# Two transposes ahead of two loads, and 22 idle products that become 14 longer ones

## The chip, the cores and the metric

The kernel runs on one core of one Trainium2 chip. The core has five engines, each with a queue of its own that is worked off in order: TensorE (PE in the profile; PEld is its loading of weights), VectorE (DVE), ScalarE (ACT), GpSimd (POOL) and SyncE (SP), which computes nothing and issues DMA transfers. Sixteen DMA engines move the data. The metric is the device time of one execution in microseconds.

## The reference: what is computed

Eight batches, eight heads, 576 positions, 64 numbers a head. First a retention (an attention with decay instead of a softmax), then a layer of 512 to 2048 to 512 with a snake activation:

```python
scores = scale * np.matmul(q, k.transpose(0, 1, 3, 2))
Dmat = np.where(rel >= 0, gamma[:, None, None] ** rel[None, :, :], 0.0)
attn = np.matmul(scores * Dmat[None], v)      # gamma: one for each head
x = attn.transpose(0, 2, 1, 3).reshape(B * S, H * D)   # 4608 x 512
h = x @ w_in                                  # 4608 x 2048
s = np.sin(alpha * h)
out = (h + s * s / (alpha + 1e-09)) @ w_out   # 4608 x 512
```

All inputs and the output are float32; the kernel multiplies in float16.

## The kernel before, in words

**Attention.** The decay is split over q and k: each is multiplied by its factors while it is cast to float16 (*cast*, line 158), so that a mask of zeros and ones is all that is left for the scores. A batch's 576 positions are two halves of 256 (p = 0 and 1) and a rest of 64 that is done for pairs of batches at the end. Each half has two chunks of 128. Within a chunk the scores are computed (*scores*, line 362), masked on DVE (*masked*) and multiplied with v (*values*, line 392). Between chunks a state of k times v is handed on: *outer* (line 295) makes the products on PE, *evict* (line 317) copies them from PSUM to the tile `kvs` on ACT, *more* (line 350) adds the decayed state of the chunk before on POOL, and *to_state* (line 341) gives the float16 form that *add_states* (line 425) multiplies with q. There is one `kvs` for all batches, so the copy of batch 3's products must wait until batch 2's last state, chunk 3, has been read from it. *keep* (line 443) copies the result to the tile `xT`.

**The layer.** A block n is 512 positions of one batch. *project* (line 541) makes 128 of the 2048 columns of h with four products of 512 columns; *sine* on ACT, *square* on ACT, DVE or POOL, and *product* on DVE turn them into a slice of `gT`; *gemm2* (line 587) adds four such slices to 128 rows of the output, and *finish* (line 581) copies and stores them. Blocks 0, 1 and 2 are interleaved with the attention of batches 1, 2, 3 and 4 by a list written out by hand (lines 653 to 1124); from block 3 on a loop of 16 units does it, with batch n + 1's attention at fixed units.

**Order.** The program is under a manual schedule: every engine gets its instructions in the order in which the calls stand in the source, and waits only for data and for buffers. So the place of a *load* (line 137, a transfer of 512 KB issued by SP) is its place in SP's queue, and the place of a *cast* on POOL its place in POOL's queue. Buffers are given out in the order of the calls from strings of slots (lines 18 to 33): `raw`, the loaded float32 data, has six slots, `k16` four, `q16` three.

**Transposes.** Batches 0 and 1 transpose k and q on PE (*turn* and *take*). From batch 2 on this is done by DMA: *crossed* (line 213) issues a DMA transpose from SBUF to SBUF of one half of k or q, 128 x 1024 float16, on SP's queue, after the cast that it reads. *scores* reads the two results, `kT` and `qT`.

**Around the change.** In the hand-written list, line 979 casts batch 3's q (second half) on POOL and lines 988 and 989 its k (first half), also on POOL. Lines 994 to 997 load and cast batch 4's k (second half) and q (first half). Then come POOL's *more(3)* of batch 2 (line 998), the transposes of batch 3's second half (lines 999 and 1000) and PE's scores on them (lines 1001 and 1003), batch 2's *to_state(3)* on POOL (line 1004), and the transposes of batch 3's first half (lines 1008 and 1009), whose first use on PE is at line 1015, behind *outer* (line 1014); *evict* is line 1016.

**Idle products.** *keep_busy* (line 602) multiplies a tile of zeros with itself into a PSUM bank that nobody reads. Line 676 issues 22 such products of 128 columns while DVE casts batch 0's q; the transposes of that q on PE (line 681) stand behind them.

Of the kernel before, what the change touches and what calls it, by code (L numbers as in the profile page):

```python
# [35 lines left out]
def kernel(  # L36
# [77 lines left out]
    def halves(n):  # L114
        return slice(64 * n, 64 * n + 64)
# [10 lines left out]
    def place(tag, shape, dtype):  # L126

        name = tag + next(slot_of[tag])
        if name not in places:
            places[name] = work.tile(shape, dtype, tag=name, bufs=1, name=name)  # L130
        return places[name]
# [5 lines left out]
    def load(b, nm, p):  # L137
        if p < 2 and b >= HALVED and nm != "q":
            t_ = place("raw", [P, H, 2 * D], F32)
            for g in range(2):  # L140
                for r in range(2):
                    s0 = 256 * p + 128 * g + 64 * r
                    nc.sync.dma_start(
                        t_[halves(g), :, r * D : r * D + D], src[nm][b, :, s0 : s0 + 64, :].rearrange("h i d -> i h d")
                    )
        elif p < 2:
            t_ = place("raw", [P, H, 2 * D], F32)
            nc.sync.dma_start(  # L148
                t_, src[nm][b, :, 256 * p : 256 * p + 256, :].rearrange("h (i r) d -> i h (r d)", r=2)
            )  # L150
        else:
            if b % 2 == 0:
                raw[b, nm, 2] = work.tile([P, H, D], F32, tag="raws", bufs=3, name=nm + "s32")
            t_ = raw[b - b % 2, nm, 2]
            nc.sync.dma_start(t_[halves(b % 2)], src[nm][b, :, 512:576, :].rearrange("h i d -> i h d"))
        raw[b, nm, p] = t_
# [47 lines left out]
    def new_T(b, nm, p):  # L204
        if (b, nm, p) not in T:
            T[b, nm, p] = (
                place(nm + "T", [P, 8, P], F16)
                if p < 2
                else work.tile([P, 4, P], F16, tag=nm + "Ts", bufs=B // 2, name=nm + "Ts")
            )  # L210
        return T[b, nm, p]

    def crossed(b, p, nms="kq"):
        for nm in nms:
            x = half[b, nm, p]
            x = x.rearrange("p a r t d -> p (a r t d)") if p < 2 else x.rearrange("p a t d -> p (a t d)")
            nc.sync.dma_start_transpose(new_T(b, nm, p), x)
# [369 lines left out]
    def gemm2(n, u, tag, cols=slice(0, 512)):  # L587
        c, part = divmod(u, 4)
        if (n, c, cols.start) not in ops:
            ops[n, c, cols.start] = psum.tile([P, 512], F32, tag=tag, bufs=1, name="ops")  # L590
        for fk in range(4 * part, 4 * part + 4):
            matmul(  # L592
                ops[n, c, cols.start][:, cols], gT[n][:, fk, c * P : (c + 1) * P], w_out16[:, fk, cols],
                start=(fk == 0), stop=(fk == FC - 1), skip_group_check=True,
            )

    at = [Attention(b) for b in range(B)]
# [4 lines left out]
    def keep_busy(n, tag, m=512):  # L602
        idle = psum.tile([P, 512], F32, tag=tag, bufs=1, name="idle")
        for _ in range(n):
            matmul(idle[:, 0:m], zero[:, 0:P], zero[:, 0:m], start=True, stop=True)
# [46 lines left out]
    with tc.manual_schedule():  # L652
# [20 lines left out]
        at[0].take_sum(0, A_)  # L673
        at[0].to_state(0, A_)
        cast(0, "q", 0, V)
        keep_busy(22, "h2", 128)
        at[0].next_sum(1)
        at[0].to_state(1, A_)
        load(0, "k", 1)
# [311 lines left out]
        gemm2(1, 2, "h2")  # L991
        gemm2(1, 3, "h2")
        at[2].keep(0, V)
        load(4, "k", 1)
        cast(4, "k", 1, G_)
        load(4, "q", 0)
        cast(4, "q", 0, G_)
        at[2].more(3)
        crossed(3, 1, "k")
        crossed(3, 1, "q")  # L1000
        at[3].scores(1, 1, "m1")
        at[3].masked(1, 1)
        at[3].scores(1, 0, "m0")
# [252 lines left out]
```

## Time and profile before

| what | value |
|---|---|
| median of 3 runs | 311.7 us (311.09 to 312.0) |
| the profiled execution | 309.53 us |
| its span, first to last instruction | 307.8 us |
| PE busy | 291.3 us, 95% |
| POOL busy | 128.9 us, 42% |
| granted TensorE clock | 1.0 |
| moved by DMA | 49.98 MB, 162 GB/s on average |

The page gives busy time for each engine, the chain of work that ended last (followed back from the last instruction to whatever released it), and groups of instructions. Its other views give the waits of each engine by what ended them, the instructions in order of time, and the busy time in chosen stretches, with the number of instructions in brackets. In these rows a line such as L372 is a line of the source, `out<-in` names the tiles, SPq is SP's queue of DMA issues, and "issue" is a wait for which the profile shows no cause. Instructions that only wait or branch are not counted in the stretches.

### The profile page before, as it was taken

Reading aid. Unit: us, or ns where it says so; the run is one execution under the profiler, and the core shown is the slowest. Engines: PE = TensorE matmul, PEld = TensorE weight load, DVE = VectorE, ACT = ScalarE, POOL = GpSimd, SP = SyncE. Lnnn points to the kernel's source line nnn. Section 1 sums busy time; section 2 is a strip of 40 time slices with the busy share of each in tenths; the row PEclk is TensorE's granted clock in tenths of the full one; section 3 lists DMA queues with packets and bytes.
Section 4 is the critical chain, followed back from the end, with each engine's and each line's share of the span. In section 5 each row is a group of like instructions: output and inputs, shape, how many; then the busy total and the mean of one; then the engine's idle time right before and its main releaser. Section 6 shows DMA issues by size and latency. Waiting matters only on the chain.

```text
span 307.8 us, 7895 instructions
## 1 busy us (share of the span) xinstructions
PE 291.3 (95%) x3225; PEld 156.3 (51%) x3225; DVE 197.2 (64%) x281; ACT 193.3 (63%) x323; POOL 128.9 (42%) x149
## 2 busy tenths in 40 slices
PE   3879999999799999999999999799999999999995
PEld 1758555555355654554455445444455454444443
DVE  2867796968576876867665686556656746655600
ACT  3748877994278668665776577556774456555411
POOL 2767774467664556686159626833030000000000
PEclk9999999999999999999999999999999999999999
DMA  8999999999567398889799969966361121111132
GB/s 222 347 224 213 275 276 324 276 235 238 126 171 207 85 182 190 234 183 150 169 255 169 205 151 269 157 142 144 75 134 38 38 43 39 34 34 34 44 90 74
DMA packets 115620, 49.98 MB, mean 162 GB/s; under 512 B 71424, under 2 KB 110592, under 8 KB 115584
## 3 DMA queue, kind: packets, MB, share of 16 engines
q1 hardware_dynamic: 112064, 45.10, 63.1%
q0 software_dynamic: 2688, 4.19, 7.6%
q8 instruction: 25, 0.41, 0.6%
q10 hardware_dynamic: 832, 0.18, 0.4%
q14 instruction: 11, 0.09, 0.1%
HBM read 36.75 MB, written 9.44 MB: 150 GB/s over the span
## 4 chain that ended last, share of the span: by engine, by line
PE 82%; DMA 7%; issue 3%; POOL 2%; ACT 2%; DVE 2%; SPq 1%; POOLq 0%; DVEq 0%; ACTq 0%
PE ops L592 38%; PE hps L549 36%; PE o L414 2%; PE sc L372 2%; DMA raw<-in_k_dram 2%; DMA raw<-in_q_dram 2%; DMA raw<-in_v_dram 2%; PE kv L308 1%; ACT s L557 1%; DMA qT<-q 1%; POOL w_in L109 1%; SPq L148 1%; PE o L436 1%; DVE ret L384 1%; POOL k L194 1%
## 5 line engine op out<-in xcount | busy, mean ns | idle before, releaser
L592 PE MATMUL ops<-w_out,gT 128*128 128x512 f16 (+2 forms) x592 | 142.6, 374 | 0.1
L557 ACT ACTIVATE s<-hps,alpha_t 128x512 f16<-128x512 f32 x144 | 97.7, 685 | 69.4 <-PE hps L549 67.9
L573 DVE SCALAR_TENSOR_TENSOR gT<-ss,inva,hps 128x512 f16<-128x512 f16 x144 | 105.6, 745 | 52.5 <-ACT ss L566 47.9
L549 PE MATMUL hps<-xT,w_in 128*128 128x512 f16 (+1 forms) x544 | 126.9, 367 | 2.1 <-issue 2.0
L549 PEld LDWEIGHTS <-w_in 128*128 128x128 f16 x608 | 68.0, 114 | 58.2 <-issue 2.2
L592 PEld LDWEIGHTS <-gT 128*128 128x128 f16 x592 | 56.2, 98 | 63.0 <-issue 0.7
L568 DVE TENSOR_TENSOR ss<-s 128x512 f16<-128x512 f16 x62 | 34.9, 562 | 20.6 <-ACT s L557 20.0
L566 ACT ACTIVATE ss<-s 128x512 f16<-128x512 f16 x73 | 46.0, 631 | 1.4
L194 POOL TENSOR_TENSOR k<-raw,cn 128x1024 f16<-128x1024 f32 (+1 forms) x17 | 26.7, 1576 | 34.0 <-DMA raw<-in_k_dram 30.0
L119 ACT COPY osb<-ops 128x512 f32<-128x512 f32 (+1 forms) x33 | 19.2, 581 | 15.2 <-PE ops L592 13.8
L384 DVE TENSOR_TENSOR ret<-sc,mask 128x1024 f16<-128x1024 f32 x20 | 23.8, 1218 | 7.1 <-PE sc L372 7.1
L194 POOL TENSOR_TENSOR q<-raw,cn 128x1024 f16<-128x1024 f32 (+1 forms) x10 | 18.5, 1868 | 2.1 <-DMA raw<-in_q_dram 1.3
L353 POOL TENSOR_TENSOR s<-kvs,cn 128x256 f32<-128x256 f32 x21 | 13.7, 651 | 11.4 <-ACT kvs L119 11.3
L354 POOL TENSOR_TENSOR kvs<-s,kvs 128x256 f32<-128x256 f32 x21 | 16.0, 762 | 3.6 <-ACT kvs L119 2.2
L119 ACT CAST xT<-o 128x1024 f16<-128x1024 f32 (+1 forms) x13 | 12.6, 983 | 7.4 <-PE o L436 7.3
L121 POOL CAST v<-raw 128x1024 f16<-128x1024 f32 (+1 forms) x11 | 11.0, 998 | 14.6 <-DMA raw<-in_v_dram 14.6
L549 PE MATMUL hps<-xS,w_in 128*128 128x512 f16 x64 | 16.4, 379 | 0.0
L178 POOL TENSOR_TENSOR ks<-ks,cn 128x512 f16<-128x512 f32 x4 | 4.2, 1044 | 22.2 <-DMA vs<-in_v_dram 13.6
L568 POOL TENSOR_TENSOR ss<-s 128x512 f16<-128x512 f16 x9 | 9.3, 1038 | 8.9 <-ACT s L557 8.9
L414 PE MATMUL o<-ret,v 64*64 64x128 f16 (+1 forms) x512 | 11.6, 215 | 1.2 <-issue 0.7
L372 PE MATMUL sc<-qT,kT 64*64 64x128 f16 (+1 forms) x512 | 10.7, 215 | 1.8 <-DVE ret L384 1.0
L372 PEld LDWEIGHTS <-kT 64*64 64x64 f16 x512 | 7.6, 107 | 8.5 <-issue 6.7
(57 smaller groups left out, 153.7 us busy)
## 6 DMA issues: line engine op xcount, KB each, us to landing
out_dram<-osb SPq DMA_DIRECT2D x70, 128.0 KB, 2.5
raw<-in_q_dram SPq DMA_DIRECT2D x16, 512.0 KB, 5.9
raw<-in_k_dram SPq DMA_DIRECT2D x10, 512.0 KB
raw<-in_v_dram SPq DMA_DIRECT2D x10, 512.0 KB, 5.7
raw<-in_v_dram SPq DMA_DIRECT2D x24, 128.0 KB, 3.3
raw<-in_k_dram SPq DMA_DIRECT2D x24, 128.0 KB, 3.4
w_in<-in_moe_w_in_dram POOLq DMA_DIRECT2D x4, 512.0 KB, 11.3
w_out<-in_moe_w_out_dram POOLq DMA_DIRECT2D x4, 512.0 KB, 11.5
```

What stands on the lines that cost most here:

```text
L119: eng.copy(d_, s_)
L194: eng.tensor_tensor(dst[:, a0:a1].rearrange("p a r t d -> p t (a r) d"), t_.rearrange("p (t a) x -> p t a x", t=2)[:, :, a0:a1].rearrange( ...
L354: nc.gpsimd.tensor_tensor(self.kvs[:, c], s32, self.kvs[:, c], ADD)
L372: matmul(sc[halves(g), t, c : c + n], kT[halves(t), 2 * a + r, halves(g)], qT[halves(t), 2 * a : 2 * a + 2, 64 * g + i0 : 64 * g + 64], st ...
L384: nc.vector.tensor_tensor(ret.rearrange("p t (z x) -> p (t z) x", z=2)[:, :, 0:n], sc.rearrange("p t (z x) -> p (t z) x", z=2)[:, :, 0:n], ...
L414: made.append(matmul(o[t][halves(e), c : c + 128].rearrange("p (r i) -> p r i", r=2)[:, :, i0:64], v16[halves(g), 4 * t + 2 * x + e, r, :] ...
L549: matmul(hps_of[n, fc][0][:, cols], w_in16[fc // 4][:, a, fc % 4 :: 4], xs[n][:, a, cols], start=(a == 0 and part != 1), stop=(a == KT - 1 ...
L557: nc.scalar.activation(s_t, hps, mybir.ActivationFunctionType.Sin, bias=0.0, scale=alpha_t[:, fc : fc + 1],)
L566: nc.scalar.activation(ss_t, s_t, mybir.ActivationFunctionType.Square)
L568: eng.tensor_tensor(ss_t, s_t, s_t, MULT)
L573: nc.vector.scalar_tensor_tensor(gT[n][:, fc, :], ss_t, inva[:, fc : fc + 1], hps, MULT, ADD)
L592: matmul(ops[n, c, cols.start][:, cols], gT[n][:, fk, c * P : (c + 1) * P], w_out16[:, fk, cols], start=(fk == 0), stop=(fk == FC - 1), sk ...
```

## The change

In the hand-written list the load and cast of batch 4's k and of batch 4's q move down by three calls, behind *more(3)* of batch 2 and behind the two transposes of batch 3's second half. SP then issues these two transposes first and the two loads after them, and POOL does *more(3)* ahead of the two casts. The casts still stand ahead of *to_state(3)*, and the loads ahead of the transposes of batch 3's first half. No buffer changes its slot, since the order of the loads among themselves, of the casts and of the transposes stays.

Apart from that, the 22 idle products of 128 columns at line 676 become 14 of 200.

```diff
         cast(0, "q", 0, V)
-        keep_busy(22, "h2", 128)
+        keep_busy(14, "h2", 200)
         at[0].next_sum(1)
...
         at[2].keep(0, V)
+        at[2].more(3)
+        crossed(3, 1, "k")
+        crossed(3, 1, "q")
         load(4, "k", 1)
         cast(4, "k", 1, G_)
         load(4, "q", 0)
         cast(4, "q", 0, G_)
-        at[2].more(3)
-        crossed(3, 1, "k")
-        crossed(3, 1, "q")
         at[3].scores(1, 1, "m1")
```

## The prediction

> **What bounds the kernel now.** I read the page first: its busy shares and its chain.
>
> ```profile
> PE 291.3 (95%) x3225; PEld 156.3 (51%) x3225; DVE 197.2 (64%) x281; ACT 193.3 (63%) x323; POOL 128.9 (42%) x149
> q8 instruction: 25, 0.41, 0.6%
> PE 82%; DMA 7%; issue 3%; POOL 2%; ACT 2%; DVE 2%; SPq 1%; POOLq 0%; DVEq 0%; ACTq 0%
> ```
>
> TensorE (PE) carries 82% of the chain that ended last and is busy for 95% of the span, so the question is where it stands still. The view of PE's waits from 21 us to the end, which I read second, is this short:
>
> ```profile
> PE hps L549 <- issue: 2.0, 1, 2.0
> PE o L436 <- issue: 1.3, 1, 1.3
> PE sc L372 <- DMA qT<-q: 0.8, 1, 0.8
> ```
>
> One more, of 0.2, is left out. The timeline of PE says where they stand (start, length, line, shape, count, idle time before):
>
> ```profile
> 19.29 0.75 PE L414 MATMUL o<-ret,v 64*64 64x128 f16 x18 [0.74 <-issue]
> ...
> 78.03 0.30 PE L436 MATMUL o<-qT,s 64*64 64x128 f16 x5 [1.27 <-issue]
> 78.26 1.90 PE L592 MATMUL ops<-w_out,gT 128*128 128x512 f16 x8
> 81.00 0.64 PE L372 MATMUL sc<-qT,kT 64*64 64x128 f16 x32 [0.84 <-DMA qT<-q]
> ...
> 194.08 0.41 PE L549 MATMUL hps<-xT,w_in 128*128 128x512 f16 x1
> 196.45 0.81 PE L549 MATMUL hps<-xT,w_in 128*128 128x512 f16 x3 [1.96 <-issue]
> 197.10 1.89 PE L592 MATMUL ops<-w_out,gT 128*128 128x512 f16 x8
> 198.82 1.03 PE L549 MATMUL hps<-xT,w_in 128*128 128x512 f16 x4
> ```
>
> An early stall at 19.29 is shown too. The stalls at 19.29, 78.03 and 196.45 wait for nothing that the profile names and fall in the middle of a run of equal products. Counting instructions explains them. Busy time by stretch, with the instructions of each engine in brackets:
>
> ```profile
> 19.10:77.90 58.80, 56.88 (x765) 33.35 (x765) 46.05 (x67) 45.01 (x82) 36.13 (x37) 1.00 1.12 255
> 77.90:196.30 118.40, 115.52 (x1402) 60.51 (x1403) 81.50 (x106) 80.87 (x130) 69.47 (x77) 1.00 0.83 184
> ```
>
> Between the first and the second stall PE takes 765 + 765 = 1530 instructions, between the second and the third 1402 + 1403 = 2805. That is 5.98 and 10.96 times 256; the sequencer's own waits and drains, which this view does not count, can make it 6 and 11. And queue q8 moves 0.41 MB in 25 packets, 16.4 KB each, for 6450 instructions of PE: 64 bytes each, 256 to a packet. So I read the three as PE running dry at a block border while q8 brings the next block. Packets of q8 stand just before two of the restarts, in the stretches 75.6 to 76.7 and 194.2 to 195.2:
>
> ```profile
> q8 instruction: 1, 0.02, 5.3%
> ...
> q8 instruction: 1, 0.02, 6.0%
> ```
>
> Each is about 1 us of one DMA engine (5.3% of 16 engines over 1.1 us), and PE restarts 1.3 to 1.4 us behind it. A border hurts only where the block before it is eaten quickly:
>
> ```profile
> 192.46:196.30 3.84, 2.03 (x140) 1.60 (x130) 2.71 (x3) 2.57 (x5) 2.79 (x4) 1.00 1.09 161
> ...
> 71.72:77.90 6.18, 4.95 (x128) 2.80 (x127) 5.23 (x6) 1.32 (x2) 4.04 (x4) 1.00 1.20 213
> 78.00:85.04 7.04, 6.16 (x127) 3.28 (x127) 3.54 (x5) 2.34 (x3) 4.04 (x5) 1.00 0.62 135
> 104.90:122.80 17.90, 17.90 (x119) 9.12 (x122) 13.29 (x19) 13.79 (x23) 11.82 (x17) 1.00 0.88 182
> ```
>
> A block of projections lasts 17.9 us, the attention block ahead of 196.45 only some 1.7 us of work (3.84 less the stall).
>
> The third view is the DMA queue of SyncE (SP), and the chain around it:
>
> ```profile
> 70.92 0.59 SPq L148 DMA_DIRECT2D raw<-in_k_dram  x1
> 71.61 0.63 SPq L148 DMA_DIRECT2D raw<-in_q_dram  x1
> 72.33 5.10 SPq L217 DMA_TRANSPOSE kT<-k  x1
> 77.54 1.29 SPq L217 DMA_TRANSPOSE qT<-q  x1
> 78.92 1.26 SPq L217 DMA_TRANSPOSE kT<-k  x1
> 80.27 1.27 SPq L217 DMA_TRANSPOSE qT<-q  x1
> ```
> ```profile
> 71.61 5.93 DMA raw<-in_q_dram
> 77.54 3.33 DMA qT<-q
> ```
>
> The transpose of k behind batch 4's two loads holds SP for 5.10 us; one with no load ahead takes 1.26. The transposed q lands 3.33 us after its issue, at 80.87, and PE starts at 81.00 on it.
>
> **The change, part by part.** The sum is made against the profiled execution, 309.53 us (span 307.8 and 1.7 around it), 0.7% under the median of 311.7.
>
> *The idle products.* 22 of 128 columns are 2816 columns, 14 of 200 are 2800, and at this point PE streams cold:
>
> ```profile
> 8.21 2.53 PE L605 MATMUL idle<-zero 128*128 128x128 f16 x22
> 10.80 0.90 PE L227 MATMUL tr<-ident,q 128*128 128x128 f16 x8
> ```
>
> The time from 8.21 to 10.80 stays, less 0.02. What changes is the count: 8 products fewer are 16 instructions fewer, so every later border falls 16 instructions, 8 products, further into the program.
>
> At 196.45: from 194.08 to 196.45 PE loses 2.37 less the pace of one product, 0.215 ((198.82 - 197.10) / 8), that is 2.15. After the change it has 8 more products of 512 columns (three projections, five of the second product) before it runs dry, 8 x 0.215 = 1.72; the block is asked for about 0.1 later (8 small products). Left: 2.15 - 1.72 + 0.1 = 0.5. Gain 1.65, between 0 (the borders are not the cause) and 2.15.
>
> At 78.03: 1.27 idle is 1.4 by start to start. 8 products further means the five left of this run and three of 78.26, 0.8 us of work; and the block's packet no longer stands behind the two loads. Left 0 to 0.9; I take 0, gain 1.4.
>
> At 19.29: PE wins up to 0.3. But SP stands still for the output weights until 31, and batch 1's loads follow:
>
> ```profile
> SPq L613 <- DMA w_out<-in_moe_w_out_dram: 18.5, 1, 18.5
> ```
>
> That transfer does not follow PE, so I cost this at 0 (up to 0.3).
>
> *The moved loads.* SP now goes from 70.92 to k's transpose at once (its cast, on DVE, stands far ahead in the code): 70.92 to 72.2. q's follows to 73.5, just behind POOL's cast of 70.27, which ends at 72.17 (row below), and lands at about 72.3 + 3.3 = 75.6, well ahead of PE. The wait at 81.00 goes: the eight products of 78.26 end their pace at 79.98, so 1.0 by start to start. Together with 78.03, PE would be 2.4 early.
>
> What is late next: the loads start at 73.6 and 74.2, 2.7 later, and the two transposes of the first half now stand behind them. The blocked one ended 6.5 after the first load's issue (72.33 + 5.10 - 70.92); so k's ends at 80.1, q's is issued at 80.15 and lands 3.33 later, 83.5. POOL's casts, that transpose's user on PE, and those behind them:
>
> ```profile
> 70.27 1.90 POOL L194 TENSOR_TENSOR q<-raw,cn 128x1024 f16<-128x1024 f32 x1
> ...
> 79.07 1.90 POOL L194 TENSOR_TENSOR q<-raw,cn 128x1024 f16<-128x1024 f32 x1 [0.84 <-POOL k L194]
> ...
> 82.42 0.61 POOL L346 TENSOR_TENSOR sS<-kvs,cn 128x256 f16<-128x256 f32 x1
> ...
> 84.88 0.53 PE L372 MATMUL sc<-qT,kT 64*64 64x128 f16 x16
> 85.12 1.01 ACT L119 COPY kvs<-kv 128x1024 f32<-128x1024 f32 x1
> ...
> 89.34 2.05 DVE L573 SCALAR_TENSOR_TENSOR gT<-ss,inva,hps 128x512 f16<-128x512 f16 x3
> ...
> 91.41 3.62 PE L549 MATMUL hps<-xT,w_in 128*128 128x512 f16 x16
> ```
>
> PE comes to 84.88 at 82.5 and waits there until 83.5: 1.0 to 1.1 of the 2.4 is given back, 0 if that transpose is held more briefly, 2.4 if longer. The next block border lies in those same scores: from 78.00 to 85.04 it had 7.0 us, and the packet came late behind transposes. With 2.4 less on the way and the same delay it would hold PE until 84.3, a give-back of 1.6. So 1.1, between 0 and 2.4.
>
> POOL takes *more(3)* ahead of the two casts instead of behind; that order alone frees nothing, since the state of chunk 3 still stands behind the casts. q's cast began 7.46 after its load's issue (79.07 - 71.61); from 74.25 that is 81.7, cast to 83.6, the state (0.61) to 84.3. ACT's copy into kvs, which must wait for it, comes at 84.3, 0.8 before 85.12. The products behind ACT free a bank at 90.0 (the first of three at 89.34) for PE's projections of 91.41, 1.4 of room: 0.8 + 1.4 = 2.2 of PE's gain fits. Cost 0. SP's later loads and stores follow PE's results and move with it.
>
> Sum: 1.4 + 1.0 - 1.1 + 1.65 = 2.95, bounds 0 and 1.4 + 1.0 + 2.15 = 4.55. The profiled execution would be at 306.6, the median at 308.7.
>
> [...]
>
> **The rivals.** *All of batch 3's gain is given back at 84.88.* For it: 5.10 us of holding, and a late packet of q8. Only 1.65 is left: 310.0. Chance 0.15.
>
> *The borders don't matter; the stalls marked issue are tied to their places.* For it: both long ones fall in attention stages. Against: multiples of 256 twice. Then the 78.03 and 196.45 stalls stay, 81.00 gives 1.0, and 84.88 is reached at 83.9, after 83.5: 310.7. Chance 0.12.
>
> *Slower: POOL holds kvs.* Batch 4's casts stand before the state of chunk 3, and ACT, in order, stands at its copy with all sines behind. To pass 0.3% (0.94) over the 1.65 won at 196.45 it must cost 2.6 beyond the 1.4 of room: the copy at 85.12 + 4.0 = 89.1, q's load landing near 86.5, 12.2 us after its issue. Against it: 7.46 was seen. At 13 us it would give 311.7 + 0.94 + 0.8 = 313.4. Chance 0.08, and 0.05 more for a run-dry that I don't see coming.
>
> **How the numbers follow.** Forecast 0.60 (307.5 to 309.6), rivals 0.15, 0.12, 0.08 and 0.05. The range takes the upper gain (4.55, 307.1, with a little for the early stall) and the first two rivals: 306.8 to 311.2, with some 0.03 left below it and 0.16 above. Anything within 0.3%, 0.94 us, can't be told from no change. Faster: 0.60 + 0.15 + half of the second rival = 0.81, less 0.04 for forecasts that fall short: 0.77. Same: the other half, 0.02 of those, and 0.02 of the two slower cases: 0.10. Slower: 0.11 of these and 0.02 of the forecasts: 0.13.
>
> **What would show it.** PE's waits lose "o L436 <- issue" and the 0.8 on qT at batch 3's first scores; an issue stall near 194.5 of about 0.5 stands eight products later, in L592; a wait of about 1 us for a transpose, or an issue stall, comes up at the scores near 83. SP shows k's transpose at 70.92 with 1.3 and the next k's with some 5. Wrong would be: stalls of the old size at the old instructions, new ones elsewhere, or ACT idle at its copy into kvs.

## The result and the profile after

The changed kernel takes 307.17 us (median of six executions, 305.71 to 309.04) beside 311.69 for the kernel before on the same chip (six, 309.82 to 312.12). The ratio is 0.9864, 95% interval 0.9823 to 0.9905, that is 4.2 us less (3.0 to 5.5). In a second set it came to 307.24 beside 310.50, 0.9898 (0.9853 to 0.9943), 3.2 us less. The pair of profiled executions lies closer together: 309.53 before, 307.47 after, 2.06 apart (spans 307.8 and 305.8). The rows that follow explain this 2.06, of one execution of each kernel; a second profile of the changed kernel, which comes out otherwise, stands behind them, and the last section comes back to the medians.

The busy time of the engines, from the page of the changed kernel:

```profile
PE 291.5 (95%) x3217; PEld 155.8 (51%) x3217; DVE 199.9 (65%) x281; ACT 193.2 (63%) x323; POOL 128.7 (42%) x149
```

PE does the same work with 8 products fewer (3217 for 3225), in a shorter span. What changed is where it stands still. Its waits from 21 us to the end (total, times, longest):

```profile
PE sc L372 <- DMA qT<-q: 0.9, 1, 0.9
PE ops L592 <- issue: 0.7, 1, 0.7
PE kv L308 <- POOL v L121: 0.3, 1, 0.3
PE hps L549 <- DMA w_in<-in_moe_w_in_dram: 0.2, 1, 0.2
```

Of the two long issue stalls of before (1.3 and 2.0) one, of 0.7, is left, in another instruction. The wait for `qT` has the old size, but the timeline of PE shows that it belongs to another transpose:

```profile
19.28 0.36 PE L414 MATMUL o<-ret,v 64*64 64x128 f16 x11 [0.30 <-issue]
...
76.53 0.51 PE L436 MATMUL o<-qT,s 64*64 64x128 f16 x24
76.97 1.90 PE L592 MATMUL ops<-w_out,gT 128*128 128x512 f16 x8
78.80 0.64 PE L372 MATMUL sc<-qT,kT 64*64 64x128 f16 x32
...
82.09 0.71 PE L308 MATMUL kv<-v,k 64*64 64x64 f16 x64
83.65 0.42 PE L372 MATMUL sc<-qT,kT 64*64 64x128 f16 x16 [0.85 <-DMA qT<-q]
...
90.27 3.62 PE L549 MATMUL hps<-xT,w_in 128*128 128x512 f16 x16
93.72 1.89 PE L592 MATMUL ops<-w_out,gT 128*128 128x512 f16 x8
95.72 1.02 PE L549 MATMUL hps<-xT,w_in 128*128 128x512 f16 x4
...
193.24 1.05 PE L549 MATMUL hps<-xT,w_in 128*128 128x512 f16 x4
194.13 1.24 PE L592 MATMUL ops<-w_out,gT 128*128 128x512 f16 x5
196.10 0.81 PE L592 MATMUL ops<-w_out,gT 128*128 128x512 f16 x3 [0.72 <-issue]
```

Read against the rows of before, by starts, this gives an account of the whole difference of these two executions:

| place | before | after | ahead by |
|---|---|---|---|
| batch 3's first scores | 81.00 | 78.80 | 2.20 |
| the scores on its first half | 84.88 | 83.65 | 1.23 |
| 16 projections | 91.41 | 90.27 | 1.14 |
| the projections behind eight L592 products | 96.59 | 95.72 | 0.87 |
| projections at the late border | 194.08 | 193.24 | 0.84 |
| span | 307.8 | 305.8 | 2.0 |

The stretch up to 81 won 2.2, the transposes of the first half took back 1.0, another 0.4 went by 96, and the late border gave 1.25. That last number: from 194.13 to 196.10 are 1.97 us for five products of 0.215, so 0.90 was lost there where 2.15 was lost before. 0.84 + 1.25 = 2.09. At 72 us PE was 0.21 later than before (72.63 for 72.42), so the work from there to the scores won 2.41.

A second profile of the same changed kernel, from a later set (305.81 us, span 304.1), is 3.72 under the profile of before, and in it PE runs through the late border:

```profile
193.34 1.89 PE L592 MATMUL ops<-w_out,gT 128*128 128x512 f16 x8
195.06 1.03 PE L549 MATMUL hps<-xT,w_in 128*128 128x512 f16 x4
```

The packet that brings the block comes earlier there. These are its rows in the DMA view of the first profile from 193.6 to 194.8 and of the second from 191.7 to 192.9:

```profile
q8 instruction: 1, 0.02, 5.0%
```
```profile
q8 instruction: 1, 0.02, 5.1%
```

Each lasts about 1 us (5% of 16 engines over 1.2 us). Narrow windows of the view give their starts. The first starts at 193.75, 2.4 behind the first product of the attention burst (191.35), and PE restarts at 196.10, 1.4 behind its end. The second starts at 191.9, only 1.4 behind its burst (190.47); 1.4 behind its end is 194.3, and PE reaches the border only at 193.34 + 5 x 0.215 = 194.4. So the second came just in time; why it came earlier is not shown. The wait for `qT` is 0.49 there for 0.85. So the table is the account of one execution and not of the kernel: the late border left 0.90 in one and nothing in the other.

SP's queue around the moved loads, from the timeline:

```profile
71.15 1.32 SPq L217 DMA_TRANSPOSE kT<-k  x1
72.58 2.19 SPq L217 DMA_TRANSPOSE qT<-q  x1
74.82 0.58 SPq L148 DMA_DIRECT2D raw<-in_k_dram  x1
75.50 0.52 SPq L148 DMA_DIRECT2D raw<-in_q_dram  x1
76.12 2.93 SPq L217 DMA_TRANSPOSE kT<-k  x1
79.14 2.39 SPq L217 DMA_TRANSPOSE qT<-q  x1
```

The transpose that held SP for 5.10 us behind the loads takes 1.32 ahead of them; the next k's, now behind the loads, takes 2.93. What stands behind the loads on POOL and ACT, from the timelines of these two:

```profile
81.82 1.90 POOL L194 TENSOR_TENSOR q<-raw,cn 128x1024 f16<-128x1024 f32 x1 [0.65 <-DMA raw<-in_q_dram]
83.68 0.80 POOL L346 TENSOR_TENSOR sS<-kvs,cn 128x256 f16<-128x256 f32 x1
84.51 1.02 ACT L119 COPY kvs<-kv 128x1024 f32<-128x1024 f32 x1 [1.63 <-POOL sS L346]
```

ACT does stand for 1.63 us at its copy into `kvs`, but the copy starts 0.6 earlier than before (85.12). In the second profile it stands for 0.18.

### The profile page after: what moved, and what is told of

The parts are those of the page before. It is cut to its first block, busy times and chain, and to the rows that moved or that the text cites. A ratio compares the mean times of both kernels' runs of the same rounds, so it can differ in the third digit from the quotient of the medians.

```text
span 305.8 us, 7881 instructions
## 1 busy us (share of the span) xinstructions
PE 291.5 (95%) x3217; PEld 155.8 (51%) x3217; DVE 199.9 (65%) x281; ACT 193.2 (63%) x323; POOL 128.7 (42%) x149
## 4 chain that ended last, share of the span: by engine, by line
PE 83%; DMA 9%; DVE 3%; issue 2%; SPq 1%; ACT 1%; POOL 1%; DVEq 0%; POOLq 0%; ACTq 0%
PE ops L592 38%; PE hps L549 37%; DMA w_in<-in_moe_w_in_dram 3%; PE o L414 2%; PE sc L372 2%; DMA raw<-in_k_dram 2%; DMA raw<-in_q_dram 2%; DMA raw<-in_v_dram 2%; PE kv L308 1%; SPq L148 1%; PE o L436 1%; DVE ss L568 1%; DVE gT L573 1%; POOL k L194 1%; DVE ret L384 0%
## 5 line engine op out<-in xcount | busy, mean ns | idle before, releaser
L592 PE MATMUL ops<-w_out,gT 128*128 128x512 f16 (+2 forms) x592 | 142.8, 374 | 0.9 <-issue 0.7
L549 PE MATMUL hps<-xT,w_in 128*128 128x512 f16 (+1 forms) x544 | 126.8, 367 | 0.3 <-DMA w_in<-in_moe_w_in_dram 0.2
L549 PEld LDWEIGHTS <-w_in 128*128 128x128 f16 x608 | 67.9, 114 | 56.7 <-issue 1.0
L592 PEld LDWEIGHTS <-gT 128*128 128x128 f16 x592 | 56.3, 98 | 63.9 <-issue 1.7
L568 DVE TENSOR_TENSOR ss<-s 128x512 f16<-128x512 f16 x62 | 37.1, 598 | 18.0 <-ACT s L557 17.4
L353 POOL TENSOR_TENSOR s<-kvs,cn 128x256 f32<-128x256 f32 x21 | 12.8, 612 | 8.6 <-ACT kvs L119 8.4
L549 PE MATMUL hps<-xS,w_in 128*128 128x512 f16 x64 | 16.4, 379 | 0.0
L119 ACT COPY kvs<-kv 128x512 f32<-128x512 f32 (+2 forms) x14 | 8.0, 573 | 7.4 <-PE kv L308 5.1
```

What stands on the lines that cost most here:

```text
L119: eng.copy(d_, s_)
L549: matmul(hps_of[n, fc][0][:, cols], w_in16[fc // 4][:, a, fc % 4 :: 4], xs[n][:, a, cols], start=(a == 0 and part != 1), stop=(a == KT - 1 ...
L568: eng.tensor_tensor(ss_t, s_t, s_t, MULT)
L592: matmul(ops[n, c, cols.start][:, cols], gT[n][:, fk, c * P : (c + 1) * P], w_out16[:, fk, cols], start=(fk == 0), stop=(fk == FC - 1), sk ...
```

## The experiments

The theory, from the prediction's counts (25 packets of q8 for 6450 instructions of PE, about 256 a packet): PE runs dry where a block of 256 instructions ends in a burst of small products, so that the number of idle products moves all later stalls; and the loads held up batch 3's transposes. The rivals: the issue stalls belong to their places and not to the count; and what the move wins is given back at the next scores. Each ratio is against executions of the kernel before in the same set, whose median is 310.12 in the set of the first four runs, 310.50 in the next and 310.02 in the last (27 products, and 32 with the loads last).

**The idle products alone.**

```diff
-        keep_busy(22, "h2", 128)
+        keep_busy(14, "h2", 200)
```

> Only the 22 idle products of 128 columns become 14 of 200; batch 4's loads stay where they were. My theory (PE runs dry at every 256th instruction when the block before was eaten fast): the same 2800 columns cost the same time, but every later border falls 8 products further. The stall at 196.45 (2.15 us from start to start) shrinks to 0.5 to 0.9 and moves eight products on, into L592; that at 78.03 (1.4) shrinks to 0 to 0.9, with the wait for qT at 81.0 taking up part of it. Gain 1.3 to 2.5 us, 309.2 to 310.4. Rival (the stalls belong to their places, the count is nothing): both stalls stand at the old instructions, gain 0, 311.7.

Measured: 308.22 us, ratio 0.9937 (0.9905 to 0.9968). Its timeline of PE:

```profile
77.09 1.90 PE L592 MATMUL ops<-w_out,gT 128*128 128x512 f16 x8
80.65 0.64 PE L372 MATMUL sc<-qT,kT 64*64 64x128 f16 x32 [1.66 <-DMA qT<-q]
...
194.37 1.24 PE L592 MATMUL ops<-w_out,gT 128*128 128x512 f16 x5
196.53 0.81 PE L592 MATMUL ops<-w_out,gT 128*128 128x512 f16 x3 [0.91 <-issue]
```

The late stall has moved by exactly the eight products, out of L549 behind its first product into L592 behind its fifth, and has shrunk from 1.96 to 0.91. So the count places the border. The stall at 78 is gone too, but that buys only 0.35: PE comes to the scores 1.2 us earlier (77.09 for 78.26), and the transpose, still behind the loads, holds them until 80.65, where before it was 81.00.

**The move alone.**

```diff
+        at[2].more(3)
+        crossed(3, 1, "k")
+        crossed(3, 1, "q")
         load(4, "k", 1)
         cast(4, "k", 1, G_)
         load(4, "q", 0)
         cast(4, "q", 0, G_)
-        at[2].more(3)
-        crossed(3, 1, "k")
-        crossed(3, 1, "q")
```

> Only the two loads and casts of batch 4 move; the idle products stay 22 of 128. My theory: the wait for qT at 81.0 goes and comes back in part (some 0.9) at the scores near 84; the stall on issue stays at the old instruction at 78 but its block no longer stands behind the loads, so there 0 to 0.9 is left; the 2.15 at 196 stays whole. Gain 1.0 to 2.0 us, 309.7 to 310.7. Rival (the move does all the work, as the measured 4.5 us against a sum of 2.95 could mean): 307 to 308, with the stall near 196 gone. Rival (the move alone is worth nothing, since what is won at 81 is waited for at 84): 311.3 to 311.9.

Measured: 308.88 us, 0.9949 (0.9916 to 0.9983). Its timeline of PE:

```profile
79.38 0.64 PE L372 MATMUL sc<-qT,kT 64*64 64x128 f16 x32
83.63 0.42 PE L372 MATMUL sc<-qT,kT 64*64 64x128 f16 x16 [0.26 <-DMA qT<-q]
...
192.73 0.41 PE L549 MATMUL hps<-xT,w_in 128*128 128x512 f16 x1
194.77 0.81 PE L549 MATMUL hps<-xT,w_in 128*128 128x512 f16 x3 [1.63 <-issue]
```

The late stall stands at its old instruction, behind the first of four, and has most of its old size (1.63 for 1.96): the move does little there. No stall is left at 78 though the border stands in its old place. The packet of that block starts at 72.9 here, at 75.6 in the kernel before and at 75.2 with the idle products alone, so it is late where the loads stand ahead of it. And what the move wins is not all given back: the scores of 84.88 stand at 83.63. Both rivals fall. PE came to the products ahead of this stretch 0.79 later than before (73.21 for 72.42) and to the scores 1.62 earlier (79.38), so the move alone wins the whole 2.41 here, as much as the whole change. The two ratios multiply to 0.9886, beside 0.9864 and 0.9898 for the whole.

**Six idle products of 467 columns**, in the changed kernel, about the same 2802 columns.

```diff
-        keep_busy(14, "h2", 200)
+        keep_busy(6, "h2", 467)
```

> The changed kernel with 6 idle products of 467 columns (2802) in place of 14 of 200: 16 instructions fewer again, the same time on PE. My theory: every border falls another 8 products further, so the stall of 0.9 that is left near 196.1 is gone (8 products of 512 columns are 1.7 us); nothing else of the size. 0.5 to 0.9 us under the changed kernel: 306.2 to 306.7. Rival (the count is nothing): 307.2, with the 0.9 still in the same place.

Measured: 306.52 us, 0.9876 (0.9836 to 0.9915), not to be told from the changed kernel by the times. The row of its timeline in which the changed kernel stalled in its first profile:

```profile
193.78 1.89 PE L592 MATMUL ops<-w_out,gT 128*128 128x512 f16 x8
```

All eight products run through without a stall: eight products further the border has a whole run of large products ahead of it. The changed kernel's second profile runs through there too, so this row alone does not show what six products are worth. Its waits show issue stalls of 0.8 near 20 us and 0.4 near 47 in exchange.

**The loads last**, behind the first half's transposes too, and their casts behind *evict* and *more(1)* of batch 3, in the changed kernel.

```diff
-        load(4, "k", 1)
-        cast(4, "k", 1, G_)
-        load(4, "q", 0)
-        cast(4, "q", 0, G_)
...
         crossed(3, 0, "q")
+        load(4, "k", 1)
+        load(4, "q", 0)
...
         at[3].more(1)
+        cast(4, "k", 1, G_)
+        cast(4, "q", 0, G_)
```

> The changed kernel with batch 4's two loads moved further down, behind the transposes of batch 3's first half too, and their casts behind POOL's first step on batch 3's state. My theory: the transpose that PE waits for near 84 (0.85 idle, 1.0 from start to start) is no longer behind the loads and that wait goes, and so does ACT's wait of 1.63 for POOL's state at its copy into kvs; batch 4's data is first needed after 106. Gain over the changed kernel 0.5 to 1.0 us: 306.2 to 306.7. Rival (the loads, later by some 2 us, make POOL's casts hold batch 3's later states, or run into the loads of 88): 307.2 to 308.5.

Measured: 306.19 us, 0.9871 (0.9828 to 0.9914). Its timelines of PE, SP and ACT:

```profile
82.50 0.42 PE L372 MATMUL sc<-qT,kT 64*64 64x128 f16 x16
...
194.45 0.81 PE L592 MATMUL ops<-w_out,gT 128*128 128x512 f16 x3 [0.64 <-issue]
```
```profile
74.70 1.26 SPq L217 DMA_TRANSPOSE kT<-k  x1
76.06 1.25 SPq L217 DMA_TRANSPOSE qT<-q  x1
77.36 2.10 SPq L148 DMA_DIRECT2D raw<-in_k_dram  x1
```
```profile
82.75 1.01 ACT L119 COPY kvs<-kv 128x1024 f32<-128x1024 f32 x1
```

With the loads out of the way both waits that the change had made are gone, PE's 0.85 at the scores and ACT's 1.63 at `kvs`; the scores start 1.15 earlier and the late border is passed 1.65 earlier (194.45 for 196.10). That late stall itself is still there (0.64). Its profiled span is 304.1, 1.7 under the first profile of the changed kernel but equal to the second, and the intervals of the two kernels overlap. So the waits go, but that the kernel is faster for it is not shown.

**The changed kernel again**, in one set with the next three.

> The changed kernel once more, beside the three below on one chip. The two parts alone gave ratios of 0.9937 and 0.9949; if they add up, 0.9886 here, some 3.5 us under the kernel before; the first measurement gave 0.9864 (0.9823 to 0.9905). My theory: 0.986 to 0.989. Rival (one part already has it all): 0.992 to 0.995.

Measured: 307.24 us, 0.9898 (0.9853 to 0.9943), just above what was expected. Its profile is the second one above.

**The loads last with 8 idle products of 350, and with 6 of 467.**

```diff
-        keep_busy(14, "h2", 200)
+        keep_busy(8, "h2", 350)
```
```diff
-        keep_busy(14, "h2", 200)
+        keep_busy(6, "h2", 467)
```

> Batch 4's loads behind all four transposes of batch 3, and 8 idle products of 350 columns (2800) in place of 14 of 200: 12 instructions fewer than the changed kernel. My theory: no wait at the scores near 83 (it was 1.0), and the stall near 194 (0.8 with the loads last and 14 products) is covered by six more products of 512 columns, 1.3 us. 0.8 to 1.8 us under the changed kernel. Rival (run-dries elsewhere take it back, as at 20 and 47 with six products): no faster than the changed kernel.

> Batch 4's loads behind all four transposes, and 6 idle products of 467 columns: 16 instructions fewer than the changed kernel. My theory: as with eight products, the stalls near 83 and 194 are gone; six products brought 1.0 at 20 and 0.55 at 47, of which the waits for batch 1's loads take up most. Within 0.5 us of the kernel with eight products, 0.8 to 1.8 us under the changed one. Rival: no faster than the changed kernel.

Measured: 305.37 us (305.29 to 305.83), 0.9843 (0.9809 to 0.9876), and 305.72 us, 0.9857 (0.9822 to 0.9892). The first is the fastest kernel of the study, 4.9 us under before (3.9 to 5.9) and 1.9 under the changed kernel's median in the same set, though the two intervals overlap a little. Its six executions lie within 0.54 us, those of the changed kernel within 3.5. Its waits of PE from 21 us on:

```profile
PE o L436 <- issue: 0.7, 1, 0.7
PE kv L308 <- DVE gT L573: 0.4, 1, 0.4
PE hps L549 <- ACT xT L119: 0.2, 1, 0.2
```

No wait for a transpose is left, and the one issue stall stands at 47 us; ahead of this view there is another of 0.8 at 20 us.

**More idle products: 32 of 88 columns, and 27 of 104**, in the changed kernel. By columns, 2816 and 2808, I put both at the time of the changed kernel's 2800 (2.52 us in its first profile); the borders move back by 36 and 26 instructions, into the attention burst ahead of the late stall's old place.

```diff
-        keep_busy(14, "h2", 200)
+        keep_busy(32, "h2", 88)
```
```diff
-        keep_busy(14, "h2", 200)
+        keep_busy(27, "h2", 104)
```

> The changed kernel with 32 idle products of 88 columns (2816): the same time on PE, but 36 instructions more, so that the borders fall 18 products earlier than in the changed kernel. My theory: borders now stand at the ends of the attention bursts near 101 and 192, where a whole block is eaten in 1.4 to 1.8 us and a quiet fetch takes 3.3 (0.9 to its packet, 1.0 of packet, 1.4 to the restart): two stalls of 1.6 to 2.7, in place of 0.9. 2 to 4.5 us slower than the changed kernel, 309 to 312. Rival (the count of idle products is nothing): as fast as the changed kernel.

> The changed kernel with 27 idle products of 104 columns (2808). With 32 of 88 no stall came at the burst near 191, and the fetch of its block stood ahead of the burst, at 190.05 to 191.2. [...] So the stall near 193 is back, inside the burst or at its end, at 1.8 to 2.6 us, and the kernel is 1 to 2 us slower than the changed one and than the one with 32: 307.5 to 309.5. Rival (that run was luck, or the count is nothing): within 0.5 us of the kernel with 32, no such stall.

Measured: 306.43 us, 0.9877 (0.9841 to 0.9914), for 32, which is a miss: I had expected it near the kernel before. For 27: 308.47 us, 0.9948 (0.9914 to 0.9981). The idle products' own time and the late burst with 32, from the timeline of PE; below it a row of the DMA view of its stretch from 189.9 to 191.3:

```profile
8.12 2.53 PE L605 MATMUL idle<-zero 128*128 128x88 f16 x32
...
190.91 0.54 PE L414 MATMUL o<-ret,v 64*64 64x128 f16 x32
...
192.38 0.47 PE L436 MATMUL o<-qT,s 64*64 64x128 f16 x16
192.78 1.05 PE L549 MATMUL hps<-xT,w_in 128*128 128x512 f16 x4
```
```profile
q8 instruction: 1, 0.02, 5.3%
```

The timeline of PE with 27:

```profile
195.02 0.36 PE L436 MATMUL o<-qT,s 64*64 64x128 f16 x12
196.29 0.25 PE L436 MATMUL o<-qT,s 64*64 64x128 f16 x4 [0.91 <-issue]
```

32 products last 2.53 us, as 22 of 128 did (0.90 ns a column, beside 0.42 for the 512-column products at 197.10), so only the count differs. With 32 there is no stall in the burst, and the block's packet starts at 190.05, 0.9 ahead of it. With 27, ten instructions further on, it starts at 193.7, 0.2 behind the start of the burst (193.54), and the burst runs dry after twelve of sixteen products and loses 0.9 (I had expected 1.8 to 2.6, an estimate that no run bears out). Why five products make this difference is not shown. By the count the border ahead of the one that stalls is near the 20th product of the burst with 27 (148 products run before the stall, less the 128 of a block), and when the packet started PE had run some 18 of them. In the two profiles of the changed kernel the packet starts 2.0 and 1.0 behind the border counted in this way (the 33rd product, at 191.72 and 190.84). So the time from border to packet is not the same in these three profiles, and what sets it is not shown.

Both kernels also wait longer for batch 2's `qT` near 73 to 75 us, 1.1 with 32 and 2.4 with 27 (which waits another 0.8 for ACT elsewhere), from the views of PE's waits of the one and the other:

```profile
PE sc L372 <- DMA qT<-q: 1.1, 1, 1.1
```
```profile
PE sc L372 <- DMA qT<-q: 2.4, 1, 2.4
```

**32 of 88 with the loads last.**

```diff
-        keep_busy(14, "h2", 200)
+        keep_busy(32, "h2", 88)
```

> Batch 4's loads behind all four transposes of batch 3, and 32 idle products of 88 columns. My theory: no run-dry near 20, 47, 78 and 192 and no wait near 83. 304.5 to 306, as fast as or up to 0.8 faster than the loads last with eight idle products (305.37), which runs dry at 20 and 47 by 0.8 to 0.9 each, mostly covered. Rival: a wait for the transposes of batch 2 (1.1 at 73 with 32 products) takes it back: 306 to 307.

Measured: 306.85 us, 0.9887 (0.9837 to 0.9936): no better than the changed kernel, as the rival had it. The wait near 74 us is 2.0 here:

```profile
PE sc L372 <- DMA qT<-q: 2.0, 1, 2.0
```

So what the late loads win is taken back there. With these counts a block's packet falls among batch 2's transposes (it starts at 70.8 with 32, 71.9 with 27 and 70.9 here). PE starts on q's transpose 4.8 to 4.9 us after its issue in these three, and at most 3.6 after it in the kernel before, which has no packet there. But with 27 and here that transpose is also issued 2.0 and 1.1 later than before (70.28 and 69.29 for 68.23). That the packet delays it is not shown, since no run moved the packet and left the rest.

## Why the prediction was right

The forecast was 308.7 by a sum of 2.95. By the ratios the kernel gained 4.2 and 3.2, by the first pair of profiles 2.06, and by the second profile of the changed kernel 3.72. So the direction was right, and the sum lies between what single executions show; whether it was too large or too small these profiles can't say. Its terms, by the first profile where nothing else is said:

- *The wait at 81.00 and the stall at 78.03 go, 2.4.* Both went; 2.20 measured, and 2.41 from 72.42 on, where PE came 0.21 late. The first two runs show what the prediction had not: each part alone removes the stall at 78.03, but the shift of borders alone then runs into the transpose and keeps 0.35, while the move alone wins all of it. The 1.4 that the sum puts down to the idle products is the move's.
- *1.1 is given back at the next transpose.* 1.0 was (2.20 to 1.23), and by that transpose: PE waited 0.85 until 83.65, where 83.5 was forecast. That the number fits is luck, for three errors cancel on the way. SP issued q's first transpose in 2.19 and not 1.3, and the loads came 1.2 later; k's next held SP for 2.93 and not for some 5, so that q's next was issued at 79.14, 1.0 before its forecast; but it landed 4.4 after its issue and not 3.33. In the second profile the give-back is 0.6 (2.01 at the scores, 1.40 at the next).
- *POOL's order costs nothing.* It held: the state ended at 84.48 (84.3 forecast) and ACT's copy began at 84.51. But ACT stood idle for 1.63 at its copy, which the prediction had named as a sign of being wrong. It was not: the copy still came 0.6 earlier than before, and no wait of PE for ACT is in the list behind it. Here too errors cancel: q's load was issued 1.25 later than forecast (75.50), and its cast began 6.32 behind it and not 7.46.
- *The late border wins 1.65, with 0.5 left.* The place was right, as the run with the idle products alone shows (1.96 at the old place, 0.91 eight products on). The size depends on the execution: 0.90 was left in the first profile, a gain of 1.25, and nothing in the second, a gain of 2.15. The forecast lies between them.
- *The early stall is worth 0 to 0.3.* The stall shrank from 0.74 to 0.30 and nothing of it was left by 69 us, where PE stood 0.2 later than before; what took it was not traced.
- *What was not in the sum:* 0.36 lost between the scores and 96 us (1.23 to 0.87), most of it ahead of 95.72, where the eight products before it end their pace at 93.72 + 8 x 0.215 = 95.44. The profile names no cause, and the second profile does not have it.

Of the rivals, the one that the borders don't matter falls by the late stall, which stood just where the count puts it with 22, 14 and 27 idle products; the one that all is given back falls by the move alone; and POOL's hold on `kvs` exists, but within the room of 2.2 that the prediction had found. The step from the profiled execution to the median was a mere shift of 0.7% in the prediction; the medians moved by more than the first pair of profiles, and came out below 308.7 (last section).

By number the stalls are few: the kernel before has 25 packets of q8 and three stalls on issue. In the late burst there was none with 32 idle products and none in the second profile of the changed kernel; it was 0.91 us with 27 and 0.72 in the first profile.

## What to carry to other kernels

Count the instructions between stalls that wait for nothing: where the count is a multiple of a block (256 by the count here), look whether the stall goes where the count sends it, as it did with 22, 14 and 27 idle products. Here 16 instructions fewer far ahead were worth as much as the rescheduling (0.9937 beside 0.9949). Where a load stands ahead of a transfer that PE will need soon, moving it behind the next such transfer passes part of the wait on (1.0 of 2.2 here); look for the place behind all of them, and move the casts with the loads. Filler work had a second price here, its number of instructions: 22 and 14 idle products take 2.53 and 2.52 us, and the late stall was 1.96 with the one and 0.91 with the other. And take more than one profile of a kernel before accounting for a microsecond: two of this one differ by 1.7.

## What the runs showed of the hardware

**A late block border lost between nothing and 2.15 us here, by its place and by the execution.** Late in the kernel the same border lost 2.15 us in the kernel before, 0.90 in one execution of the changed kernel and nothing in another, nothing with six or with 32 idle products, and 0.91 (idle before the restart) with 27.

**The granted clock dips in some executions.** Of the 53 executions of the kernel before that count in the ratios of the experiments, 24 had a mean granted clock below 0.9965, and in each of the three sets these were the longer ones: medians 311.5, 311.2 and 311.5 us, against 309.6, 309.8 and 309.8 for the others. Of the changed kernel it was 2 of 12, with the loads last or with six idle products 1 of 30, with only the idle products changed 3 of 12, with 27 or 32 of them (loads not last) 7 of 22, with only the move 6 of 12. Where a profile caught one, with only the move, the windows show it in 8 us of the first attention work (the column before the last two is the clock):

```profile
16.00:20.00 4.00, 3.21 (x66) 2.62 (x69) 2.51 (x3) 1.01 (x1) 3.83 (x6) 0.66 1.23 217
20.00:24.00 4.00, 3.83 (x92) 2.95 (x81) 2.30 (x5) 2.49 (x4) 0.56 (x2) 0.92 1.24 208
```

At a full clock the changed kernel's executions have medians of 307.1 and 307.7 in its two sets, some 2 to 2.7 under the 309.8 of before, near the 2.06 of the first pair of profiles. So the larger differences of the medians go with fewer dips. But the second profile of the changed kernel has a dip of the same size in the same place (0.66 and 0.91 in these two windows), and that execution took 305.8. And at a full clock the changed kernel still runs from 305.5 to 309.0; the late border, which cost 0.90 in one profile and nothing in the other, is one thing that varies. Why one kernel has more dips, and where they fall in the kernel before, stays open: its profile has none.
